# A dilated-attention and mixture-of-experts kernel: another order of the last tiles, weight sums one step earlier, last rows scaled by two engines

## The chip, the core and the metric

The kernel runs on one core of a Trainium2 chip. The core has five engines with their own instruction queues: TensorE (PE; its weight loads are shown as PEld), VectorE (DVE), ScalarE (ACT), GpSimd (POOL) and SyncE (SP). In this kernel SP issues the plain loads and stores, and POOL issues the indirect ones (gathers and scatters by a list of row numbers). The metric is the device time in microseconds of one execution.

## What is computed

Two stages follow each other. First attention over 8 batches and 8 heads, 576 positions, 64 values per head, with a plain window of 32 for half of the heads and a dilated one for the others. Its result is the input `x` of a mixture of experts: every token goes through one expert of eight, and the choice can be carried over from the token before.

```python
for b in range(B):                                   # B, S, D, E, F = 8, 576, 512, 8, 1024
    prev_e = -1
    for s in range(S):
        fresh_e = int(np.argmax(logits[b, s]))       # logits = x @ w_gate
        if s == 0 or local_gate[b, s] < 0.5:         # local_gate = sigmoid(x @ w_local)
            e = fresh_e
        else:
            e = prev_e if prev_e >= 0 else fresh_e
        prev_e = e
        p = softmax(logits[b, s])                    # in short
        h = np.maximum(x[b, s] @ w1[e], 0.0)
        out[b, s] = p[e] * (h @ w2[e])
```

All data is 32-bit floating point.

## The kernel before

**Stages.** The loop at L1155 runs the attention. Near its end the routing starts: which tokens go to which expert. When half of the batches are routed, two early units of tokens can begin; the rest of the routing runs between their matmuls. From `run_hidden(0, [])` (L1264) on, TensorE works on the experts only.

**Units.** Tokens of one expert are packed into units of fixed kinds, and only the expert numbers and token lists are data. Unit 0 is "plain" (two tiles of 128 tokens), unit 1 an early "pair". Units 2 to 17 take their kinds from `ORDER` (L85): a quad is four tiles of 128 tokens, a pair two, a full one, a half one tile of up to 64 tokens, a few one of up to 32. The n-th full in `ORDER` takes the n-th full tile in the order of the experts, and so for each kind; moving a kind within `ORDER` does not change which tokens it gets.

**One unit's work.** `features(u)` (L898) transposes the gathered tokens (TensorE L907, ScalarE copies L908). `hidden(u)` (L942) is the first layer with relu, `output(u)` (L1033) the second layer, a scaling by the gate's probability, and `send` (L1028, POOL L1029), which scatters the rows to their places in `out`. Every send writes `out`, and so waits until the send before has landed.

**Quads and pairs** use a scheme with seven block products instead of eight (Strassen's, in Winograd's form; `chain`, L916). It needs sums of blocks, made by VectorE: four of the inputs (`xc` or `xcq`, L860 to L863 by way of `sums_right`), four of the first-layer weights (`sums[0]`, L854 to L857 by way of `sums_left`), four of the second-layer weights (`sums[1]`, L860 to L863) and four of the hidden values (`hc`, L854 to L857). One operation on weights is 128x1024. The products go to three PSUM accumulators x, y, z; product 7 writes x again after x was read behind product 5 (`finish(3)`). In the first layer `finish` is VectorE L1008 and a relu (L1009, L1006), in the second VectorE L1104 or ScalarE L1101; `keep` is ScalarE L1000 or L1097.

**The order of a step.** From unit 2 on, step u issues: `hidden(u)`, `features(u+1)`, `gather(u+2)`, `output(u-1)`. So the output of a unit comes one step after its first layer. The order on every engine is the order in which the Python program issues its instructions. VectorE's sums and the routing's steps are woven between matmuls: `work_gap` is called after each group of matmuls; it runs a routing step from `waiting` if there is one, and one or two sums from the list `soon`. What is handed to `run_hidden(u, push)` or `run_output(u, push)` is put on `soon`, and what is left is issued at its end (`flush`). `both(u)` (L1241) gives the four `hc` sums of a pair or quad, woven with its four `sums[1]` unless `early_sums` (L1248) has issued those in the unit's own first layer; it does so for a quad that doesn't follow a pair.

**Weights.** There are two slots for each layer's weights, `raw1[0]`, `raw1[1]`, `raw2[0]` and `raw2[1]`, 2 MB each. Quads and the first pair use slot 0, the others slot 1. `weights(u, second)` (L803) is issued on SP's queue as soon as the slot's last user is done, and it moves nothing if the slot holds that expert already (L817).

**The first two units and the end** are written out by hand. These are the lines that the change rewrites:

```python
run_hidden(0, [])
push = features(1)
run_output(0, sums_of_weights(1, False) + push)
run_hidden(1, sums_of_weights(1, True))
```

In them the first-layer sums of unit 1 and its four `xc` sums are issued in unit 0's output, and the second-layer sums of unit 1 in its own first layer. The routing steps of that time are, in this order: `fresh` (L478 to L499), `carry` (TensorE L507, VectorE L509 and L511), `carry_over` (TensorE L517, VectorE L519 to L522), `carry_in` (TensorE L527, VectorE L528), `choose` (TensorE L533, VectorE L537 to L547), `gate` (L555 to L561), `place` (TensorE L571 and L572, VectorE L574), `lanes_of`, `matrices` (L580 to L614), `products` (TensorE L623), `count` (TensorE L640, VectorE L643 to L729), `table` (TensorE L739) and `late_tokens` (TensorE L756, VectorE L766 to L781), after which the gathers of unit 2 are issued. At the end, the last unit (17) is a quad.

Of the kernel before, what the change touches and what calls it, by code (L numbers as in the profile page):

```python
# [14 lines left out]
Act = mybir.ActivationFunctionType  # L15
Alu = mybir.AluOpType
# [8 lines left out]
D = H * DH  # L25
# [19 lines left out]
FEED = 4  # L45
# [36 lines left out]
QUADS, PAIRS, FULL, HALF, FEWS = 6, 2, 4, 1, 3  # L82
C_FULL, C_HALF, C_FEW = (2 * MOST + k * E for k in range(3))
COLS = C_FEW + E
ORDER = ("pair", "full", "quad", "few", "half", "quad", "full", "few", "quad", "full", "few", "quad", "pair", "quad",  # L85
         "full", "quad")
assert [ORDER.count(kind) for kind in ("quad", "pair", "full", "half", "few")] == [QUADS, PAIRS, FULL, HALF, FEWS]
assert 4 * QUADS + 2 * PAIRS <= C_FULL

# [133 lines left out]
def whole(ctx, tc, exact, bad, qk, v, wgl, w1, w2, con, adm, msk, qmk, out, cst, wg, ones, warm):  # L223
    nc = tc.nc
# [562 lines left out]
    else:  # L787
        kinds = list(ORDER)
    cols = dict(quad=(0, 4), pair=(0, 2) if exact else (2 * MOST - 2, -2), full=(C_FULL, 1), half=(C_HALF, 1), few=(C_FEW, 1))
# [3 lines left out]
    NU = len(units)  # L793

    def of_unit(u, what, j=0, rows=P):
        return tiles[what, units[u]["late"]][:rows, units[u]["col"] + j:units[u]["col"] + j + 1]
# [22 lines left out]
    waiting, soon = [], []  # L819
# [3 lines left out]
    def gap(add=None):  # L823
        if add is not None:
            credit[0] = min(credit[0] + add, add)
        alone = False
        while waiting and not alone and (add is None or credit[0] >= 0):
            f, cost, _ = waiting.pop(0)
            credit[0] -= cost
            if f:  # L830
                f()
            alone = add is None or not waiting or waiting[0][2]

    def work_gap(sums=True):
        before = credit[0]
        gap()
        for _ in range(len(soon) > 4 and 2 or len(soon) > 0 if sums and before - credit[0] < 1.2 else 0):
            soon.pop(0)()
# [5 lines left out]
    def flush():  # L844
        while soon:
            soon.pop(0)()

    def quarter(w, i, k, second):
        if second:
            return w[:, FK // 2 * i:FK // 2 * (i + 1), D // 2 * k:D // 2 * (k + 1)]  # L850
        return w[:, FK // 2 * i:FK // 2 * (i + 1), DK // 2 * k:DK // 2 * (k + 1)]
# [7 lines left out]
    def sums_right(to, b11, b12, b21, b22):  # L859
        return [lambda: nc.vector.tensor_tensor(to[:, 0], b12, b11, op=Alu.subtract),  # L860
                lambda: nc.vector.tensor_tensor(to[:, 1], b22, to[:, 0], op=Alu.subtract),
                lambda: nc.vector.tensor_tensor(to[:, 2], b22, b12, op=Alu.subtract),
                lambda: nc.vector.tensor_tensor(to[:, 3], b21, to[:, 1], op=Alu.subtract)]  # L863

    def sums_of_weights(u, second):

        i = units[u]["slot"]
        assert (u, second) in loads
        if second:
            return sums_right(sums[1], *(quarter(raw2[i], k, j, True) for k in range(2) for j in range(2)))  # L870
        return sums_left(sums[0], *(quarter(raw1[i], f, k, False) for f in range(2) for k in range(2)))
# [6 lines left out]
    def rows_in(u):  # L878
        return dict(half=ROW, few=FEW).get(units[u]["kind"], P)
# [153 lines left out]
    def output(u):  # L1033
        i, kind = units[u]["slot"], units[u]["kind"]
        h, w = ht.pop(u), raw2[i]
        if kind in ("half", "few"):
            rows = rows_in(u)
            parts, n = P // rows, FK * rows // P
            yp = bank([P, D // parts], "yp")
            hh = h[:, 2:2 + n // 2].rearrange("p m (c t) -> p (m c) t", t=P)  # L1040
            for m in range(FK):
                for v in range(parts):
                    nc.tensor.matmul(yp[v * rows:(v + 1) * rows],
                                     lhsT=hh[:, m % n, m // n * rows:(m // n + 1) * rows],
                                     rhs=w[:, m, v * D // parts:(v + 1) * D // parts], start=(m == 0),
                                     stop=(m == FK - 1), tile_position=(0, v * rows), skip_group_check=True)
                if m % 2:
                    yield True
            y = stage.tile([P, D], F32, name="y", bufs=3)
            nc.vector.tensor_scalar(y[:, :D // parts], yp, of_unit(u, "gate"), None, Alu.mult)  # L1050
            c = units[u]["col"] - C_HALF
            nc.gpsimd.indirect_dma_start(
                out=out.rearrange("n (v f) -> (n v) f", v=parts),
                out_offset=bass.IndirectOffsetOnAxis(ap=tiles["side"][:, c:c + 1], axis=0),
                in_=y[:, :D // parts], in_offset=None, bounds_check=parts * N - 1, oob_is_err=False)
            return
        if kind == "plain":
            for j in range(2):
                yp = bank([P, D], "yp")
                for m in range(FK):  # L1060
                    nc.tensor.matmul(yp, lhsT=h[:, m, j * P:(j + 1) * P], rhs=w[:, m], start=(m == 0), stop=(m == FK - 1))
                    if m % 2:
                        yield True
                y = stage.tile([P, D], F32, name="y", bufs=3)
                nc.scalar.activation(y, yp, Act.Copy, scale=of_unit(u, "gate", j))
                send(y, u, j)
            return
        if kind == "full":
            yp = bank([P, D], "yp")
            for m in range(FK):  # L1070
                nc.tensor.matmul(yp, lhsT=h[:, m, :P], rhs=w[:, m], start=(m == 0), stop=(m == FK - 1))
                yield True
            y = stage.tile([P, D], F32, name="y", bufs=3)
            nc.vector.tensor_scalar(y, yp, of_unit(u, "gate"), None, Alu.mult)
            send(y, u, 0)
            return
        half = D // 2
        for q in range(tiles_of(u) // 2):
            if q:
                now(sums_left(hc, *blocks(h, q)))  # L1080
            xyz = [bank([P, half], "yp") for _ in range(3)]
            ys = [stage.tile([P, D], F32, name="y", bufs=3) for _ in range(2)]

            def product(to, a, b, first):
                for m in range(FK // 2):
                    nc.tensor.matmul(to, lhsT=a[:, m], rhs=b[:, m], start=first and m == 0,  # L1086
                                     stop=(m == FK // 2 - 1), skip_group_check=True)

            def at(k):
                return ys[k // 2][:, k % 2 * half:(k % 2 + 1) * half]  # L1090

            def gate(k):
                return of_unit(u, "gate", 2 * q + k // 2)

            def keep(k, of):
                k = (0, 1, 3)[k]
                nc.scalar.activation(at(k), of, Act.Copy, scale=gate(k))  # L1097

            def finish(k, of):
                if k == 2:  # L1100
                    nc.scalar.activation(at(k), of, Act.Copy, scale=gate(k))  # L1101
                    send(ys[1], u, 2 * q + 1)
                else:
                    nc.vector.scalar_tensor_tensor(at(k), of, gate(k), at(k), Alu.mult, Alu.add)  # L1104
                    if k == 1:
                        send(ys[0], u, 2 * q)

            yield from chain((lambda j, k: blocks(h, q)[2 * j + k], lambda s: hc[:, s]),
                             (lambda k, j: quarter(w, k, j, True), lambda s: sums[1][:, s]),
                             *xyz, product, keep, finish)  # L1110
# [109 lines left out]
    def run_hidden(u, push):  # L1220
        soon.extend(push)
        for fits in hidden(u):
            work_gap(fits)
        if not units[u]["late"] and units[u]["kind"] == "pair":
            now(units[u]["sums"][:2])
        flush()
        if after[u] is not None and u >= FIRST:
            weights(after[u], False)

    def run_output(u, push):  # L1230
        soon.extend(push)
        for fits in output(u):
            work_gap(fits)
        flush()
        if after[u] is not None and u >= FIRST:
            weights(after[u], True)
# [24 lines left out]
        now(features(FIRST))  # L1261
        gather(FIRST + 1)

    run_hidden(0, [])  # L1264
    push = features(1)
    run_output(0, sums_of_weights(1, False) + push)
    run_hidden(1, sums_of_weights(1, True))
    soon.extend(units[1]["sums"][2:])
    rest = output(1)
    for k in range(FEED + 2):  # L1270
# [5 lines left out]
    for u in range(FIRST, NU):  # L1276
# [5 lines left out]
        push = sums_of_weights(u + 1, False) if is_pair(u + 1) else both(u) if u + 1 == NU else []  # L1282
# [67 lines left out]
```

## Time and profile before

| what | value |
|---|---|
| median of three runs | 658.38 us (657.23 to 659.29) |
| the profiled execution | 656.34 us, its span 654.6 us, granted clock 0.996 |
| VectorE and ScalarE busy | 323.0 us (49%), 193.7 us (30%) |
| POOL busy | 172.9 us (26%) |
| TensorE waits from 149 us to its end | four, 2.3 us together |
| DMA, mean over the span | 180 GB/s, 117.83 MB |
| weight loads issued | 36 of 2048 KB (some of them skipped), 4 of 512 KB |
| VectorE, one sum of weights (128x1024) | 1.22 us |
| VectorE, one 128x512 scaling from PSUM (L1074) | 0.75 us |
| ScalarE, one 128x256 scaling from PSUM (L1101) | 0.47 us |

The span runs from the first to the last instruction; the execution's time has 1.7 us more around it. TensorE's matmuls are pipelined and their ends are modelled, so TensorE shown busy is not TensorE at its peak. In a timeline row the first number is the start in us from the span's start, the second the length in us, and square brackets hold the idle time of that engine just before, with what ended it. In the list of waits the numbers are the total in us, how often, and the longest.

### The profile page before, as it was taken

To read this page: it belongs to the slowest core of one execution; us is meant where nothing else is said; L and a number is where in the kernel's file an instruction comes from. 1 tells how busy PE (TensorE), PEld (TensorE's weight loads), DVE (VectorE), ACT (ScalarE), POOL (GpSimd) and SP (SyncE) were. 2 spreads that over 40 slices of the span, in tenths; PEclk is the share of its full clock that TensorE was granted. 3 is DMA by queue.
4 is the path that set the end of the run, shared out by engine and by line. 5 is a ranking of instruction groups with operands and counts; after the bars stand their busy time and mean duration, and the time that the engine had idled before them with its cause. 6 is when DMAs were issued, how large, how long until landed. Compare 5 with 4: busy or idle time off the path is not lost. (4 is left out here: it accounts for less than half of the span.)

```text
span 654.6 us, 13525 instructions
## 1 busy us (share of the span) xinstructions
PE 637.7 (97%) x5602; PEld 542.1 (83%) x5602; DVE 323.0 (49%) x727; ACT 193.7 (30%) x364; POOL 172.9 (26%) x169
## 2 busy tenths in 40 slices
PE   8999999989999999999999999999999999999995
PEld 6988888878587998777889868986899888988784
DVE  3558588683696663232632363125466422742420
ACT  3555444551113322311431123212333132212210
POOL 3322213251204622051405130513531241111011
PEclk9999999999999999999999999999999999999998
DMA  8999898849101364284816170817255243404001
GB/s 314 338 298 318 296 289 309 254 123 389 55 34 49 106 253 165 93 349 153 338 60 274 49 298 10 314 45 288 81 225 212 82 159 145 161 33 157 0 31 53
DMA packets 32102, 117.83 MB, mean 180 GB/s; under 512 B 8637, under 2 KB 17053, under 8 KB 28576
## 3 DMA queue, kind: packets, MB, share of 16 engines
q1 hardware_dynamic: 25232, 97.66, 41.4%
q0 software_dynamic: 6800, 19.21, 8.6%
q8 instruction: 46, 0.75, 0.5%
q14 instruction: 24, 0.20, 0.1%
HBM read 116.86 MB, written 19.20 MB: 208 GB/s over the span
## 5 line engine op out<-in xcount | busy, mean ns | idle before, releaser
L1029 POOL DMA_INDIRECT out_dram<-y,tok x36 | 44.0, 1223 | 262.8 <-DVE y L1104 99.4
L1086 PE MATMUL yp<-sum,hc 128*128 128x256 f32 x360 | 82.7, 379 | 0.6 <-DVE hc L854 0.6
L1104 DVE SCALAR_TENSOR_TENSOR y<-yp,gate,y 128x256 f32<-128x256 f32 x45 | 21.8, 483 | 114.7 <-issue 75.7
L1086 PEld LDWEIGHTS yp<-sum,hc 128*128 128x128 f32 x360 | 68.3, 190 | 10.3 <-DVE hc L854 1.0
L995 PE MATMUL hp<-xcq,sum 128*128 128x256 f32 x288 | 64.1, 379 | 0.0
L995 PEld LDWEIGHTS hp<-xcq,sum 128*128 128x128 f32 x288 | 54.7, 190 | 7.4
L891 POOL DMA_INDIRECT xg<-xd,tok x40 | 43.5, 1089 | 62.0 <-PE tp L907 34.2
L284 POOL COPY vt<-vt 32x1040 f32<-32x1040 f32 x32 | 35.8, 1121 | 90.8 <-DMA vt<-in_v_dram 64.6
L339 PE MATMUL two<-kq 64*96 64x64 f32 x1152 | 53.5, 243 | 0.0
L339 PEld LDWEIGHTS two<-kq 64*96 64x96 f32 x1152 | 53.3, 162 | 0.1
L1008 DVE TENSOR_TENSOR hq<-hp,hq 128x512 f32<-128x512 f32 x36 | 24.8, 690 | 52.6 <-PE hp L995 52.6
L1086 PE MATMUL yp<-raw,hq 128*128 128x256 f32 x192 | 45.7, 381 | 0.0
L891 POOL DMA_INDIRECT xg<-xd,pos x40 | 40.6, 1016 | 11.8 <-issue 11.1
L995 PE MATMUL hp<-xeq,raw 128*128 128x256 f32 x192 | 43.5, 380 | 0.0
L390 PE MATMUL pv<-vt,pr 96*64 96x65 f32 x1152 | 41.2, 224 | 1.2 <-POOL vt L284 1.0
L390 PEld LDWEIGHTS pv<-vt,pr 96*64 96x64 f32 x1152 | 36.5, 137 | 5.1 <-issue 1.6
L344 DVE SCALAR_TENSOR_TENSOR pr<-two,mk 96x512 f32<-96x512 f32 x32 | 21.9, 685 | 37.8 <-ACT pr L346 26.6
L1086 PEld LDWEIGHTS yp<-raw,hq 128*128 128x128 f32 x192 | 36.1, 190 | 5.3 <-issue 0.5
L995 PEld LDWEIGHTS hp<-xeq,raw 128*128 128x128 f32 x192 | 36.2, 190 | 4.8
L1097 ACT ACTIVATE y<-yp,gate 128x256 f32<-128x256 f32 x45 | 21.3, 473 | 63.6 <-PE yp L1086 58.7
L1009 ACT ACTIVATE hq<-hq 128x512 f32<-128x512 f32 x36 | 22.7, 630 | 44.1 <-DVE hq L1008 44.1
L1101 ACT ACTIVATE y<-yp,gate 128x256 f32<-128x256 f32 x15 | 7.1, 473 | 91.2 <-PE yp L1086 91.2
(260 smaller groups left out, 1048.7 us busy)
## 6 DMA issues: line engine op xcount, KB each, us to landing
raw<-in_w_dram SPq DMA_DIRECT2D x36, 2048.0 KB
kq<-in_qk_dram SPq DMA_DIRECT2D x32, 592.0 KB
vt<-in_v_dram SPq DMA_DIRECT2D x32, 292.5 KB
xd<-x SPq DMA_DIRECT2D x16, 512.0 KB
raw<-in_w_dram SPq DMA_DIRECT2D x4, 512.0 KB
xd<-x SPq DMA_DIRECT2D x32, 32.0 KB
xg<-xd,tok POOLq DMA_INDIRECT x40, 4.0
xg<-xd,pos POOLq DMA_INDIRECT x40, 3.7
```

The lines of the kernel that those rows point to most:

```text
L284: nc.gpsimd.tensor_copy(vt[:WIN, :, 1:], vt[QB:, :, :NB - 1])
L339: nc.tensor.matmul(sc[:KW, u, k * QB:(k + 1) * QB], lhsT=kt[h, i * QB:i * QB + KW], rhs=qt[h, i * QB:(i + 1) * QB], start=bool(late), stop ...
L344: nc.vector.scalar_tensor_tensor(pr, sc[:KW, :, :w], -CEIL, mk[:, kind].unsqueeze(1).to_broadcast([KW, 2, w]), Alu.max, Alu.min)
L390: nc.tensor.matmul(to[h * QB:(h + 1) * QB], lhsT=pr[i][:, u], rhs=vt[:, u, i], start=True, stop=True, tile_position=(0, h * QB), skip_grou ...
L891: nc.gpsimd.indirect_dma_start(out=x[:rows, g], out_offset=None, in_=xd[g] if units[u]["late"] else xd[g][:EARLY * GS], in_offset=bass.Ind ...
L995: nc.tensor.matmul(to[part][:, m_], lhsT=a[:, m, kk], rhs=b[:, kk], start=first and m_ == 0 and kk == 0, stop=(kk == DK // 2 - 1), skip_gr ...
L1008: nc.vector.tensor_tensor(to, of[part], to, op=Alu.add)
L1009: nc.scalar.activation(to, to, Act.Relu)
L1029: nc.gpsimd.indirect_dma_start(out=out, out_offset=bass.IndirectOffsetOnAxis(ap=of_unit(u, "tok", j), axis=0), in_=y, in_offset=None, boun ...
L1086: nc.tensor.matmul(to, lhsT=a[:, m], rhs=b[:, m], start=first and m == 0, stop=(m == FK // 2 - 1), skip_group_check=True)
L1097: nc.scalar.activation(at(k), of, Act.Copy, scale=gate(k))
L1104: nc.vector.scalar_tensor_tensor(at(k), of, gate(k), at(k), Alu.mult, Alu.add)
```

## The change

Three things are changed. In `ORDER`, the full and few tiles from the seventh place on stand in other places: a few now comes ahead of the second full, the third few moves from the eleventh place to the fourteenth, and a full is last, after the last quad. The counts of each kind stay as they are. The four sums of unit 1's first-layer weights are put on `soon` in unit 0's first layer, behind group 4 (`FEED`), and those of its second-layer weights follow the `xc` sums in unit 0's output; nothing is handed to unit 1's first layer. Where the last unit is a full tile, VectorE scales its first 256 columns and ScalarE the other 256; other full tiles are scaled by VectorE alone, as before.

```diff
-ORDER = ("pair", "full", "quad", "few", "half", "quad", "full", "few", "quad", "full", "few", "quad", "pair", "quad",
-         "full", "quad")
+ORDER = ("pair", "full", "quad", "few", "half", "quad", "few", "full", "quad", "full", "quad", "pair", "quad", "few",
+         "quad", "full")
...
             y = stage.tile([P, D], F32, name="y", bufs=3)
-            nc.vector.tensor_scalar(y, yp, of_unit(u, "gate"), None, Alu.mult)
+            left = D // 2 if u + 1 == NU else D
+            nc.vector.tensor_scalar(y[:, :left], yp[:, :left], of_unit(u, "gate"), None, Alu.mult)
+            if left < D:
+                nc.scalar.activation(y[:, left:], yp[:, left:], Act.Copy, scale=of_unit(u, "gate"))
             send(y, u, 0)
...
-    run_hidden(0, [])
+    for k, fits in enumerate(hidden(0)):
+        if k == FEED:
+            soon.extend(sums_of_weights(1, False))
+        work_gap(fits)
+    flush()
     push = features(1)
-    run_output(0, sums_of_weights(1, False) + push)
-    run_hidden(1, sums_of_weights(1, True))
+    run_output(0, push + sums_of_weights(1, True))
+    run_hidden(1, [])
```

## The prediction

> **What bounds the kernel now.** I read the page's part 1 first, then who waited for whom with TensorE as the waiting engine, window by window, then VectorE's timeline around the waits found, and last the chain that ended last together with the timeline of the final 10 us.
>
> ```profile
> span 654.6 us, 13525 instructions
> ...
> PE 637.7 (97%) x5602; PEld 542.1 (83%) x5602; DVE 323.0 (49%) x727; ACT 193.7 (30%) x364; POOL 172.9 (26%) x169
> ```
>
> TensorE is busy 97% of the span. Its work is the same in both kernels (same matmuls, other order), so only its stalls and the two ends can give time. From 149 us to the end the waits of TensorE are these four, and from 250 to 640 us there is none:
>
> ```profile
> PE hp L995 <- DVE h L1008: 0.8, 1, 0.8
> PE yp L1086 <- DVE hc L854: 0.6, 1, 0.6
> PE ep L739 <- DVE chosen_late L729: 0.4, 1, 0.4
> PE hp L995 <- DVE sum L854: 0.4, 1, 0.4
> ```
>
> All four lie in units 1 and 2 (182 to 215 us). VectorE's timeline shows the cause of the first two (start, length, line):
>
> ```profile
> 194.82 1.22 DVE L861 TENSOR_TENSOR sum<-raw,sum 128x1024 f32<-128x1024 f32 x1
> 195.96 0.69 DVE L1008 TENSOR_TENSOR h<-hp,h 128x512 f32<-128x512 f32 x1
> 196.56 1.22 DVE L862 TENSOR_TENSOR sum<-raw 128x1024 f32<-128x1024 f32 x1
> 197.69 0.68 DVE L1008 TENSOR_TENSOR h<-hp,h 128x512 f32<-128x512 f32 x1
> ...
> 200.94 1.22 DVE L863 TENSOR_TENSOR sum<-raw,sum 128x1024 f32<-128x1024 f32 x1
> 202.08 0.69 DVE L854 TENSOR_TENSOR hc<-h 128x512 f32<-128x512 f32 x1
> ```
>
> Unit 1's second-layer weight sums (L861 to L863, 1.22 us each) stand in VectorE's queue ahead of the steps that TensorE waits for: two sums before the second L1008, one before the first hc. The tail, from the timeline of the end and the chain:
>
> ```profile
> 645.85 0.99 POOL L1029 DMA_INDIRECT out_dram<-y,tok  x1 [7.42 <-DVE y L1104]
> 646.75 0.47 ACT L1101 ACTIVATE y<-yp,gate 128x256 f32<-128x256 f32 x1 [6.43 <-PE yp L1086]
> 649.65 0.98 POOL L1029 DMA_INDIRECT out_dram<-y,tok  x1 [2.81 <-issue]
> ```
> ```profile
> 645.85 2.76 DMA out_dram<-y,tok
> ```
>
> TensorE ends at 646.71 (the last ACT starts 0.04 later). The last rows are scaled at 647.22, but their send starts only at 649.65: each send waits until the one before has landed (645.85 + 2.76 = 648.61) plus about 1 us. From the last send's start to the span's end it is 4.9 us.
>
> **Part 1, the sums one step earlier.** Nothing is added: the same eight operations of 1.22 us move. L854 to L857 go into unit 0's first layer, between the routing steps; L860 to L863 take their place in unit 0's second layer, all ahead of L710.
>
> New place of the first four: VectorE idles there, as the waits of its own rows show:
>
> ```profile
> 161.75 0.34 DVE L511 TENSOR_TENSOR_SCAN run<-row 12x96 f32<-12x96 f32 x1
> ...
> 163.32 0.16 DVE L520 COPY ends<-last 1x11 f32<-1x11 f32 x1 [1.22 <-PE last L517]
> ...
> 165.37 0.26 DVE L528 TENSOR_SCALAR run<-run,op 12x96 f32<-12x96 f32 x1 [1.69 <-PE op L527]
> 167.44 0.17 DVE L537 TENSOR_SCALAR ei<-cp 96x12 int32<-96x12 f32 x1 [1.80 <-PE cp L533]
> ```
>
> L854 starts when slot 1's first-layer weights are there. Three weight loads leave at 148.38, 149.35 and 149.97; their landing events end at 157.28, 162.21 and 167.08, one after another, and L854 needs the second. So L854 runs 162.25 to 163.47, then L519 to L522 to about 163.9, and TensorE's L527 at 165.14 doesn't wait: 1.3 us of slack. L855 ends at 165.1 (L528 needs 165.37), L856 at 166.8 (L537 needs 167.44), L857 follows L547 and ends at 169.7, L561 then at 170.9, before L571 on TensorE at 171.70. Cost: 0. If the load were late, see the third rival.
>
> Saving, followed through the queue. Before L643, VectorE now has 4 x 0.42 + 2 x 1.22 = 4.1 us of moved work instead of 4 x 1.22 + 2 x 0.42 = 5.7, so L643 starts when TensorE's count is there, about 182.7 instead of 183.23. Up to L729 the inserted work grows from 1.8 to 2.3 us (steps of 1.14, since neighbours overlap a little): L729 ends 0.06 earlier, 194.85. From there L1008, L1008, L741, L1008 follow without sums: the second L1008 ends at 196.1 instead of 198.37, and the wait of 0.85 before product 7 goes. The token steps after the third L1008 end at about 199.6 instead of 201.04; hc (L854) starts when ScalarE's last relu is done, 200.25, ends 200.94, and TensorE wants it at 201.13: the second wait goes too (0.77 between TensorE's due start 202.05 and its start at 202.82). Sum: 0.06 + 0.85 + 0.77 = 1.7 us. The gathers of unit 2 leave with the token steps, 1.4 us earlier; their second tile landed at 208.62 for transposes that begin at 209.83 and now begin at 208.1 with the landing at 207.2: covered. The wait of 0.42 on unit 2's sum moves along unchanged. Bounds: 0 and 2.1 (0.85 + 0.77 + 0.44); I take 1.7.
>
> **Part 2, the order of the tiles.** By the routing of these inputs unit 15 (few) and full 3 share an expert, and the second pair now stands between them, so slot 1's two weight arrays are loaded once more, some 4 MB. Loads cost TensorE nothing while they land before use; alone they take 8 to 9 us here (589.80 to 598.48), behind another up to 12.6 (483.17 to 495.77), and the shortest cover in the new order is unit 16's first layer: unit 13's output (12.1), few (1.9) and transposes (1.8), 15.8 us. Price 0. Few and full 2 exchange places with the same expert: no load.
>
> The new neighbourhood quad, few, quad (units 14 to 16) loads VectorE. Between unit 13's output and unit 14's it has eight sums (557.21 to 564.24 for the same eight before the old unit 16), four xcq (568.19 to 570.73) and three weight sums (570.73 to 574.33). Counted from the end of unit 13's output, T0 (558.27 there), the first two blocks end at T0 + 5.97 and + 8.5, the weight sums at + 12.1, then L1104, L857, L1104 end at + 14.3. Before, a full tile of 7.1 us gave cover; now TensorE starts output 14 at T0 + 3.6 and wants the second L1104 done at product 7, T0 + 3.6 + 10.36 = 13.96. A stall of 0.3; bounds 0 and 1.2 (one more 1.22 us sum in front). At the few-to-quad step (unit 10) the first sum is ready 6.5 us after the transposes begin, wanted at 7.1: no cost.
>
> **Part 3, the tail.** After TensorE's end the full tile has one send, and the quad's last is 7.6 us away, landed and free about 1 us before. So the wait of 649.65 - 647.22 - 0.27 goes. The scaling of 128x512 by VectorE takes 0.75 (L1074), 128x256 0.485 (L1050, the half tile), by ScalarE 0.47. In the built order of the changed kernel the ScalarE half waits for the count that the VectorE half raises, so they run one after the other: 0.04 + 0.485 + 0.04 + 0.473 = 1.04, then 0.27 to the send (645.57 to 645.85): 1.31 us after TensorE's end, where it is now 2.94. Saving 1.63. Bounds: side by side 0.8, saving 2.1; the send still behind a landing, saving 0.
>
> The Trainium skill (PSUM — Partial Sum Buffer, PSUM bank collisions raise a hardware error) says that two engines must not read one bank and quadrant at once, reads against reads included, and that the compiler therefore orders them. No run here shows a collision. By that rule the split costs more than VectorE alone (1.04 against 0.79), which speaks against it; if reads could overlap, the tail would be 0.5 us shorter.
>
> **Sum.** -1.7 + 0.3 - 1.63 = -3.0. The profiled execution took 656.34 us (span 654.6, 1.7 around it): 653.3 in its terms. The median of the runs shown, 658.38, lies 2.04 above that execution, so I forecast 655.4, own range 653.6 to 656.4.
>
> **The rivals.**
> 1. The early waits only change place, because the routing chain on VectorE (L643 to L729, nearly gapless) sets the pace anyway. For: ep waits for L729 and gains 0.06. Against: both other waits have sums directly in front. Time: 658.38 - 1.63 + 0.3 = 657.1. Chance 0.13.
> 2. The halves run side by side and the jam at unit 15 doesn't appear: 655.4 - 0.5 - 0.3 = 654.6. Against: the wait in the built order. Chance 0.10.
> 3. The slower one: the first-layer weights of slot 1 land late and L854 blocks the routing steps queued behind it (L520, L522), for which TensorE's L527 and all matmuls after it wait. It decides from a landing at 163.5 on and eats the whole gain from 163.5 + 3.0 = 166.5. With the loads interleaved, so that the second lands with the third at 167.08, TensorE loses 3.7: 659.1; 1.3 us later still it is over 0.3%. Against: the landings 5 us apart. Chance 0.07, 0.05 of it beyond 0.3%.
> 4. The reorder does not free the last send: it still waits for the quad's. Time 657.0. Against: 7.6 us between them, 3.8 us per send. Chance 0.08.
>
> **How the numbers follow.** Forecast 0.62. About 0.3% (2.0 us) is what a measurement of this kernel can tell from no change: faster means below 656.4. Faster: 0.62 + 0.10 = 0.72; within: 0.13 + 0.08 + 0.02 = 0.23; slower 0.05. The range must hold rivals 1, 2 and 4 with the spread of the runs (about 1 us either way): 652.6 to 657.8.
>
> **What would show it.** No wait of L995 on L1008 and of L1086 on hc near 198 to 203 us, L854 beginning right at 162.2, a wait of about 0.3 us in unit 14's output, the last ACT row beginning where the last DVE row ends, and 6.2 us from TensorE's end to the span's. Wrong would be: a wait of TensorE on L522 near 165 us, any wait on a weight load after 500 us, or two sends in the last 5 us.

## The result and the profile after

| what | before | after |
|---|---|---|
| median of 6 runs each, side by side | 657.87 us (657.05 to 659.66) | 654.39 us (653.10 to 656.56) |
| ratio to the kernel before, 95% interval | | 0.9945 [0.9922, 0.9967] |
| the profiled execution, its span | 656.34, 654.6 us | 656.56, 654.8 us |
| first product of unit 0's first layer (L964) | 149.49 | 153.19 |
| from there to product 2 of unit 1's output | 53.33 us | 51.69 us |
| from there to TensorE's end | 443.89 us | 443.42 us |
| TensorE's end to the last send | 2.94 us | 1.35 us |
| TensorE's end to the span's end | 7.85 us | 6.47 us |
| DMA | 117.83 MB | 122.02 MB |

The kernel became 3.5 us faster (2.2 to 5.1 by the interval). The two profiled executions do not show it at first sight: their spans are alike, because the one of after was the slowest of its six runs. The windows of the trace tell why. First the kernel before, then after; the columns are the stretch in us, its length, the busy time of PE, PEld, DVE, ACT and POOL with their counts, the granted clock, the DMA share and GB/s.

```profile
120.00:146.00 26.00, 24.32 (x473) 20.74 (x470) 19.28 (x77) 13.00 (x26) 11.18 (x15) 1.00 0.61 189
146.00:200.00 54.00, 52.52 (x334) 39.98 (x333) 35.43 (x127) 10.80 (x21) 8.05 (x6) 1.00 0.38 146
```
```profile
120.00:146.00 26.00, 23.68 (x471) 20.33 (x468) 19.36 (x77) 12.78 (x25) 9.01 (x13) 1.00 0.67 199
146.00:200.00 54.00, 53.50 (x343) 40.78 (x344) 37.89 (x130) 10.64 (x21) 8.09 (x9) 0.97 0.39 148
```

The last column but two is what to look at: in the run of after the granted clock was 0.97 between 146 and 200 us. That is the mean over one stretch of 3.41 us at half clock (147.03 to 150.44), which lies ahead of unit 0's first product and can hold TensorE up by 1.7 us; the attention stage, whose instructions the change does not touch, had run late already. Unit 0's first product came 3.7 us later. So the two kernels are compared from that product on: 505.07 us to the span's end before, 501.6 after, 3.5 us less, which agrees with the runs. The 3.5 are 1.64 in the early units, 0.47 in the long middle and 1.38 at the end.

The waits of TensorE between 150 and 250 us, in the list of after (total us, how often, longest):

```profile
PE ep L739 <- DVE chosen_late L729: 0.5, 1, 0.5
PE hp L995 <- DVE sum L854: 0.4, 1, 0.4
```

Of four rows two are left: the waits on L1008 and on `hc` are gone. From 250 us to 640 us the list is empty, as before. VectorE and TensorE at the place where the first sums went, from the timeline of after (start, length, engine, line, operation):

```profile
165.45 0.34 DVE L511 TENSOR_TENSOR_SCAN run<-row 12x96 f32<-12x96 f32 x1
165.82 1.23 DVE L854 TENSOR_TENSOR sum<-raw 128x1024 f32<-128x1024 f32 x1
...
166.82 0.17 PE L517 MATMUL last<-cst,run 12*1 12x12 f32 x1
...
167.02 0.16 DVE L520 COPY ends<-last 1x11 f32<-1x11 f32 x1
167.21 0.17 DVE L522 TENSOR_TENSOR_SCAN over<-ends 1x12 f32<-1x12 f32 x1
...
168.84 0.19 PE L527 MATMUL op<-ones,over 1*12 1x1 f32 x2
```

L854 begins as its weights are complete (the last of the load's sixteen parts landed at 165.80). L522 is done at 167.38, and L527 starts at 168.84 without a wait behind its name: the sum fitted. The tail, from the timeline of the end and then from the chain that ended last:

```profile
648.34 0.48 DVE L1075 TENSOR_SCALAR y<-yp,gate 128x256 f32<-128x256 f32 x1 [8.04 <-PE yp L1071]
648.90 0.48 ACT L1077 ACTIVATE y<-yp,gate 128x256 f32<-128x256 f32 x1 [6.96 <-DVE y L1075]
649.65 0.98 POOL L1029 DMA_INDIRECT out_dram<-y,tok  x1 [2.85 <-ACT y L1077]
```
```profile
640.57 4.20 DMA out_dram<-y,tok
...
645.81 2.73 DMA out_dram<-y,tok
...
649.65 0.98 POOL out_dram L1029
```

TensorE ends at 648.30. The ScalarE half begins 0.08 us after the VectorE half has ended (its releaser is L1075), and the last send follows the ScalarE half (releaser L1077). The chain, though, shows how little cover there was: the quad's two sends took 4.20 and 2.73 us, and the second landed only at 648.54.

### The profile page after: what moved, and what is told of

Same layout as the page of the kernel before. It is cut to its first block, busy times and chain, and to the rows that moved or that the text cites. A ratio compares the mean times of both kernels' runs of the same rounds, so it can differ in the third digit from the quotient of the medians.

```text
span 654.8 us, 13519 instructions
## 1 busy us (share of the span) xinstructions
PE 639.5 (98%) x5602; PEld 543.3 (83%) x5602; DVE 324.1 (49%) x727; ACT 194.6 (30%) x365; POOL 169.6 (26%) x169
## 2 busy tenths in 40 slices
DMA packets 32390, 122.02 MB, mean 186 GB/s; under 512 B 8669, under 2 KB 17085, under 8 KB 28608
## 5 line engine op out<-in xcount | busy, mean ns | idle before, releaser
L1029 POOL DMA_INDIRECT out_dram<-y,tok x36 | 41.0, 1140 | 244.5 <-DVE y L1107 90.5
L1107 DVE SCALAR_TENSOR_TENSOR y<-yp,gate,y 128x256 f32<-128x256 f32 x45 | 21.8, 483 | 101.2 <-issue 70.5
L1008 DVE TENSOR_TENSOR hq<-hp,hq 128x512 f32<-128x512 f32 x36 | 24.9, 691 | 42.6 <-PE hp L995 42.6
```

The source lines that it names most:

```text
L1008: nc.vector.tensor_tensor(to, of[part], to, op=Alu.add)
L1029: nc.gpsimd.indirect_dma_start(out=out, out_offset=bass.IndirectOffsetOnAxis(ap=of_unit(u, "tok", j), axis=0), in_=y, in_offset=None, boun ...
```

## The experiments

The kernel before took 658.85 us on the chip of E1 to E4, called the first here (E12 ran on it too, at 659.08), 666.41 on the second (E5 to E8) and 662.65 on the third (E9 to E11). So a kernel is compared only through its ratio to the kernel before in runs on the same chip, and, closer, by stages of its profile:

| kernel | ratio, 95% interval | unit 0's first product to unit 1's product 2 | to TensorE's end | TensorE's end to last send | to the span's end |
|---|---|---|---|---|---|
| before, after | , 0.9945 [0.9922, 0.9967] | 53.33, 51.69 | 443.89, 443.42 | 2.94, 1.35 | 7.9, 6.5 |
| E1 sums only | 0.9989 [0.9972, 1.0006] | 51.67 | 443.78 | 3.19 | 8.0 |
| E2 order and split | 0.9963 [0.9944, 0.9981] | 53.33 | 443.50 | 1.35 | 6.4 |
| E3 order only | 0.9957 [0.9932, 0.9982] | 53.32 | 443.54 | 1.08 | 6.0 |
| E4 no split | 0.9946 [0.9928, 0.9964] | 51.68 | 443.40 | 1.10 | 6.0 |
| E5 late load | 1.0006 [0.9984, 1.0029] | 52.93 | 451.19 | 1.36 | 6.2 |
| E6 two banks | 0.9932 [0.9906, 0.9958] | 51.70 | 449.55 | 0.84 | 6.1 |
| E7 sums first | 0.9934 [0.9914, 0.9954] | 51.13 | 449.30 | 1.35 | 6.5 |
| E8 two banks, sums first | 0.9929 [0.9901, 0.9958] | 51.13 | 449.58 | 0.84 | 6.2 |
| E9 after again | 0.9939 [0.9914, 0.9964] | 52.01 | 445.31 | 1.36 | 6.4 |
| E10 sums first, no split | 0.9914 [0.9880, 0.9948] | 51.12 | 447.17 | 1.07 | 6.0 |
| E11 extra sum | 0.9935 [0.9905, 0.9964] | 51.69 | 446.61 | 1.36 | 6.5 |
| E12 late load, old sums | 0.9955 [0.9937, 0.9973] | 53.33 | 443.49 | 1.36 | 6.2 |

**E1, the sums alone.** The order and the scaling of the kernel before, with only this:

```diff
-    run_hidden(0, [])
+    for k, fits in enumerate(hidden(0)):
+        if k == FEED:
+            soon.extend(sums_of_weights(1, False))
+        work_gap(fits)
+    flush()
     push = features(1)
-    run_output(0, sums_of_weights(1, False) + push)
-    run_hidden(1, sums_of_weights(1, True))
+    run_output(0, push + sums_of_weights(1, True))
+    run_hidden(1, [])
```

> The kernel before with only the sums of unit 1's weights made one step earlier; order and tail stay. My theory: the two waits of TensorE at 198 and 203 us (0.85 and 0.77) go and nothing takes their place, so the time is 1.7 us below the kernel before (ratio 0.9974), and from the first product of unit 0's first layer to product 2 of unit 1's output it is 51.7 us instead of 53.3. Tail as before: last send 2.9 us after TensorE's end. Rival (early waits only change place): the same time as before within 0.4 us (ratio 0.9994 to 1.0), with a new wait of TensorE in that stretch or after it.

The early stage took 51.67 us, 1.66 less, and the middle stayed. The ratio alone cannot tell the theory (0.9974) from the rival (0.9994 and up): both lie in its interval. The runs differ by the clock granted to them, 0.989 to 0.999, and E1's happened to have less of it (mean 0.9942, the kernel before 0.9956). A least-squares fit over the 82 runs of E1 to E4 and of the kernel before beside them, with one term for each kernel and one for (1 - clock) x 655 us, gives that last term a factor of 0.81 and puts E1 at -2.06 us (plus or minus 0.64) against the kernel before, E2 at -1.95 (0.63), E3 at -1.75 (0.66) and E4 at -3.34 (0.63). The mean clock also counts what lies behind TensorE's end, where it costs nothing: in the profile of before the only stretch at half clock begins at 649.66, and TensorE ends at 646.71. E1 and the kernel before have tails of like length, and so have E3 and E4, which differ by the same edit (1.6 us apart by the fit); these comparisons stand. E2 to E4 against the kernel before have tails 1.5 us shorter and so come out some 0.6 us too small (an estimate: 0.81 times half of 1.5). So the sums bring their 1.7, which the stage shows directly, and the first rival falls. E1 and E2 together, -4.0, make up the whole change within the intervals.

**E2, order and split without the early sums**, E1's edit undone in the changed kernel.

> The changed kernel without the early sums: new order and split last rows only. My theory: 1.4 to 2.1 us below the kernel before (ratio 0.9968 to 0.9979), all of it behind 640 us: last send 1.3 us after TensorE's end instead of 2.9; the waits of 0.85 and 0.77 near 200 us are there as before; the middle between them is within 0.5 us of the kernel before. Rival (the reorder costs a stall in units 14 to 16): a gain of only 0.3 to 1.0 us and a wait of TensorE between 550 and 600 us. Rival (the tail gains nothing, the last send still waits for the quad's): a gain of under 0.5 us.

Ratio 0.9963, 2.4 us faster. The early stage is that of before to the hundredth, and TensorE's waits from 150 to 660 us are, in E2's list:

```profile
PE hp L995 <- DVE h L1008: 0.8, 1, 0.8
PE yp L1089 <- DVE hc L854: 0.6, 1, 0.6
PE ep L739 <- DVE chosen_late L729: 0.4, 1, 0.4
PE hp L995 <- DVE sum L854: 0.4, 1, 0.4
```

The same four as before, and no fifth in units 14 to 16: the new order itself costs no stall there.

**E3, the order alone**, and **E4, the change without the split.** Both have this, E4 with the early sums, E3 without:

```diff
-            left = D // 2 if u + 1 == NU else D
-            nc.vector.tensor_scalar(y[:, :left], yp[:, :left], of_unit(u, "gate"), None, Alu.mult)
-            if left < D:
-                nc.scalar.activation(y[:, left:], yp[:, left:], Act.Copy, scale=of_unit(u, "gate"))
+            nc.vector.tensor_scalar(y, yp, of_unit(u, "gate"), None, Alu.mult)
```

> The kernel before with only the new order: VectorE alone scales the last rows (128x512). My theory: the order carries the whole tail gain and the split costs 0.25: the last send starts 1.06 us after TensorE's end (0.04 + 0.75 + 0.27) instead of 1.3 with the split, unless the quad's landing is what releases it; time 1.6 to 2.3 us below the kernel before, and the same or 0.25 below the run with the split. Rival (the split carries a part of the gain): 0.2 us or more slower than the run with order and split.

> The changed kernel with the last rows scaled by VectorE alone. My theory: the ScalarE half starts only when the VectorE half has ended, so leaving the split out brings the last send from 1.35 to about 1.06 us after TensorE's end; time 0.25 us below the changed kernel, or the same where the quad's last landing releases the send. Rival (the halves overlap in effect and the split pays): 0.3 us or more slower than the changed kernel.

E4's tail, from its timeline, with TensorE's end at 645.90:

```profile
643.48 0.99 POOL L1029 DMA_INDIRECT out_dram<-y,tok  x1 [4.32 <-issue]
...
645.93 0.75 DVE L1074 TENSOR_SCALAR y<-yp,gate 128x512 f32<-128x512 f32 x1 [8.04 <-PE yp L1071]
647.00 0.98 POOL L1029 DMA_INDIRECT out_dram<-y,tok  x1 [2.53 <-DVE y L1074]
```

One operation of 0.75 us in place of 0.48 + 0.08 + 0.48: the last send comes 1.10 us after TensorE's end, 0.25 earlier than with the split; in E3 1.08. To the span's end it is 6.0 us in both against 6.4 and 6.5. The order has all of the tail's gain, and the split takes 0.25 of it back at the last send. Whether it also costs the other 0.2 is not shown: from the last send to the span's end the runs with this split take 4.87 to 5.15 us, those with VectorE alone 4.90 to 4.96. The times can't show so little: E4's ratio is that of the changed kernel.

**E5, a late load**, for the third rival: what happens when the sum's weights come late.

```diff
         if n == NPB + 1:
             weights(0, True)
-            weights(1, False)
...
     weights(1, True)
+    weights(1, False)
```

> The changed kernel with the first-layer weights of slot 1 asked for behind its second-layer weights, so that they land some 5 us later (about 14 to 17 us after TensorE begins unit 0's first layer, instead of 12.6). Third rival of the prediction as a theory: the first sum then stands in VectorE's queue waiting for the landing and blocks the routing steps queued behind it (L520, L522), for which TensorE's L527 and all matmuls after it wait; TensorE loses 3 to 4.5 us there and the time is 3 to 4.5 us above the changed kernel. Rival (the scheduled place has slack enough, or the sums don't block): the same time as the changed kernel within 0.5 us, no wait of TensorE at L527.

The gain is gone: ratio 1.0006. The timeline of E5, at the same place as that of after above (unit 0's first product at 154.36):

```profile
169.61 1.23 DVE L854 TENSOR_TENSOR sum<-raw 128x1024 f32<-128x1024 f32 x1 [2.65 <-DMA raw<-in_w_dram]
...
170.76 0.15 DVE L520 COPY ends<-last 1x11 f32<-1x11 f32 x1
...
170.94 0.17 DVE L522 TENSOR_TENSOR_SCAN over<-ends 1x12 f32<-1x12 f32 x1
...
171.26 0.18 PE L527 MATMUL op<-ones,over 1*12 1x1 f32 x2 [1.19 <-DVE over L522]
```

VectorE stands 2.65 us before the sum, waiting for the weights; L520, whose input had come from TensorE at 168.15, is queued behind; and TensorE waits 1.19 us for L522. The early stage is 1.24 us longer than in the changed kernel. The mechanism is the rival's. The size in this profile is smaller than expected: the load landed 4.9 us behind the one before it (164.70 and 169.59), as expected, but only 15.2 us after unit 0's first product, 2.6 later than in after (12.6).

The runs lost more than that 1.24. The fit used for E1, over the 63 runs of this chip (factor 0.82), puts E5 at -0.42 us (0.80) against the kernel before and E6 to E8 at -3.90 to -4.09. The profile has two stretches at half clock; these rows of its windows lie inside them (columns as above):

```profile
150.70:154.00 3.30, 3.30 (x32) 1.34 (x31) 1.66 (x3) 0.52 (x2) 1.45 (x2) 0.50 0.99 266
300.90:304.20 3.30, 3.30 (x10) 2.59 (x9) 1.60 (x3) 0.47 (x1) 0.75 (x2) 0.50 0.21 79
```

The second, 300.86 to 304.28, is why the middle is 1.6 us longer than in E6, whose waits of TensorE there are the same. The first, 150.68 to 154.09, seems to hide a part of the loss: the first of the three loads left at 151.01, unit 0's first product came 3.35 us behind it, and in the eight profiles without a stretch at half clock near that place it is 1.1 to 1.7. With these the sum would have begun 16.9 to 17.5 us after the first product, and TensorE would have waited 2.9 to 3.4 us (an estimate, by the threshold of 14.06 worked out below). That is about what the runs lost, since by stages E6 to E8 are 0.4 to 0.9 us better than the changed kernel; no profile shows it.

**E12, the late load with the sums in their old places**, to see whether the transfers' order costs something by itself.

> The load of slot 1's first-layer weights asked for late, as in the run with the late load, but the sums of unit 1's weights left in their old places; new order and split tail stay. The run with the late load gave up about 4 us against the changed kernel, of which its profile shows 1.24 at L527. My theory (only the blocked routing steps cost): no wait at L527, the late load by itself is free, and the time is that of the run with order and split without the early sums, ratio to the kernel before 0.9963 (0.9944 to 0.9981). Rival (the late load itself costs, by the order of the transfers and not by what stands behind the sum): ratio 0.998 to 1.001, with a longer stage before unit 0's first product or a new wait of TensorE behind it.

Ratio 0.9955, early stage 53.33, no wait at L527: the late load is free where no sum stands in front of the routing. It was another chip than E5's.

**E6, two banks for the last output**: two products of 256 columns each, VectorE scales the first while TensorE makes the second, ScalarE scales that.

```diff
+            if u + 1 == NU:
+                for c in range(2):
+                    cols = slice(c * D // 2, (c + 1) * D // 2)
+                    yp = bank([P, D // 2], "yp")
+                    for m in range(FK):
+                        nc.tensor.matmul(yp, lhsT=h[:, m, :P], rhs=w[:, m, cols], start=(m == 0), stop=(m == FK - 1))
+                        yield True
...
```

> The changed kernel with the last full tile's output as two products of 256 columns in two PSUM banks: VectorE scales the first half while TensorE computes the second, ScalarE scales the second. My theory: one bank shared by the two engines is what made the halves run one after the other; with two banks 0.04 + 0.47 + 0.27, so the last send starts about 0.8 us after TensorE's end instead of 1.35, and the time falls by up to 0.5 us. TensorE's own time is the same or up to 0.3 longer (16 matmuls of 256 columns instead of 8 of 512). Rival (the quad's last landing releases the send, not the rows): ScalarE ends 0.5 us earlier, the send starts at the same distance from the quad's landing, gain under 0.2 us.

```profile
647.87 0.99 POOL L1029 DMA_INDIRECT out_dram<-y,tok  x1 [2.78 <-issue]
648.46 0.48 DVE L1080 TENSOR_SCALAR y<-yp,gate 128x256 f32<-128x256 f32 x1 [4.63 <-PE yp L1075]
651.96 0.47 ACT L1078 ACTIVATE y<-yp,gate 128x256 f32<-128x256 f32 x1 [6.48 <-PEq L218]
652.71 0.98 POOL L1029 DMA_INDIRECT out_dram<-y,tok  x1 [3.84 <-ACT y L1078]
```

In E6's timeline the VectorE half (L1080) is done three microseconds before the ScalarE half begins, 0.09 after TensorE's end at 651.87. The last send is 0.84 us after TensorE's end, as expected, and TensorE's output takes 7.07 us against 7.03. But the end of the span is 6.1 us after TensorE's end, 0.4 less than in after and no better than without the split (E3 and E4): in this profile what is won at the send is given back in its landing. Nor could the send have gone much sooner: the quad's second send had landed only at 651.68, and where the rows are long ready a send starts 1.04 us after the landing before it (before: 648.61 and 649.65).

**E7, the second-layer sums ahead of the token sums**, and **E8**, E6 and E7 together.

```diff
-    run_output(0, push + sums_of_weights(1, True))
+    run_output(0, sums_of_weights(1, True) + push)
```

> The changed kernel with unit 1's four second-layer weight sums put ahead of the token sums of unit 1 in unit 0's output. My theory: the last wait of TensorE in that stretch (0.5 us on L729, which ends late because two weight sums of 1.22 us stand among the routing steps from L643 to L729) becomes shorter or goes, since only two steps of 0.42 us then stand there: 0.3 to 0.5 us below the changed kernel. Rival (the chain from L643 to L729 is bound by TensorE and its round trips, not by the sums): the wait of 0.5 stays, same time within 0.2 us. A third outcome: the token sums come late for unit 1's first products, with a new wait of TensorE there, and the time is 0.3 us or more above.

> The changed kernel with both further edits, last output in two PSUM banks and the weight sums ahead of the token sums. My theory: the two gains lie in different stretches and add, 0.5 to 1.0 us below the changed kernel. Rival (neither end is what binds): within 0.3 us of the changed kernel.

In E7's list of waits from 150 to 250 us one row is left:

```profile
PE hp L995 <- DVE sum L854: 0.4, 1, 0.4
```

The wait on L729 is gone, and the early stage is 0.56 us shorter (51.13 against 51.69). By stages E7 is 0.5 us better than the changed kernel; by ratios (0.9934, E8 0.9929, the changed kernel 0.9945 and 0.9939 on other chips) this is not resolved.

**E9 to E11, side by side on a third chip**: the changed kernel again (E9), E7's edit without the split (E10), and the changed kernel with one of unit 16's sums made twice (E11):

```diff
         push = sums_of_weights(u + 1, False) if is_pair(u + 1) else both(u) if u + 1 == NU else []
+        if u + 3 == NU:
+            push = push[:1] + push
```

> The changed kernel itself once more, as the measure for the runs beside it on the same chip. My theory: ratio to the kernel before 0.9945 as measured at first (0.9922 to 0.9967), tail from TensorE's end to the end of the span 6.4 to 6.5 us, no TensorE wait in units 14 to 16. Rival: what the first profile showed was luck, and a wait of some 0.3 us in unit 14's output comes and goes.

E9 repeats the gain (0.9939), and it shows something that the first profile did not. From its timeline, with unit 0's first product at 150.76:

```profile
165.08 1.23 DVE L854 TENSOR_TENSOR sum<-raw 128x1024 f32<-128x1024 f32 x1 [1.73 <-DMA raw<-in_w_dram]
...
166.42 0.17 DVE L522 TENSOR_TENSOR_SCAN over<-ends 1x12 f32<-1x12 f32 x1
...
166.74 0.18 PE L527 MATMUL op<-ones,over 1*12 1x1 f32 x2 [0.26 <-DVE over L522]
```

The third rival's wait is here in the changed kernel itself, 0.26 us long. Fifteen of the load's sixteen parts had landed by 162.48, the last at 165.06. The loads before and behind it have a last part as late (2.4 and 2.6 us).

> The changed kernel with unit 1's second-layer weight sums ahead of the token sums in unit 0's output, and the last rows scaled by VectorE alone. My theory: 0.55 us saved before 202 us (the wait on L729 goes) and 0.25 at the last send: 0.5 to 1.0 us below the changed kernel (ratio to it about 0.9988), and the best of all versions run. Rival (the end of the span hangs on landings, not on the send): only 0.3 to 0.6 below.

E10 has the lowest ratio of all, 0.9914, its median 0.9 us below E9's; the intervals overlap. By stages it gains 0.89 in the early units (0.32 of that is the wait above and its neighbours, which E9 had on this chip) and 0.4 at the end, and in its profile waits of 1.5 and 0.3 us in middle quads take that back. So by its interval it beats the kernel before; that it beats the changed kernel is likely and not shown.

> The changed kernel with one more VectorE sum (128x1024, 1.22 us, the first of unit 16's first-layer sums made twice; the result is the same) ahead of the others in unit 14's output. In the changed kernel's trace the second L1107 of that output ended at 569.06 and TensorE's product behind it started at 569.20, so the jam on VectorE missed TensorE by 0.14 us. My theory (the jam is real and nearly decides): TensorE waits 1.0 to 1.1 us on L1107 there, and the time is 0.7 to 1.2 us above the changed kernel. Rival (TensorE has more room there, since products go on in other banks): no wait over 0.2 us, same time.

Unit 14's output on VectorE and TensorE, from the timelines of after and then of E11:

```profile
567.46 1.21 DVE L857 TENSOR_TENSOR sum<-raw,sum 128x1024 f32<-128x1024 f32 x1
568.59 0.47 DVE L1107 SCALAR_TENSOR_TENSOR y<-yp,gate,y 128x256 f32<-128x256 f32 x1
...
569.20 1.91 PE L1089 MATMUL yp<-sum,hq 128*128 128x256 f32 x8
```
```profile
568.71 1.21 DVE L857 TENSOR_TENSOR sum<-raw,sum 128x1024 f32<-128x1024 f32 x1
569.84 0.87 DVE L1107 SCALAR_TENSOR_TENSOR y<-yp,gate,y 128x256 f32<-128x256 f32 x2
...
570.37 1.99 PE L1089 MATMUL yp<-sum,hq 128*128 128x256 f32 x8 [1.03 <-DVE y L1107]
```

The second L1107 starts 1.25 us later, and TensorE waits 1.03 us for it. So the jam is real, and the changed kernel misses it by little more than a tenth of a microsecond. In the times the difference (0.9935 against 0.9939) is not resolved.

## Why the prediction came out right, point by point

**What bounds the kernel.** TensorE, and its stalls in units 1 and 2 and the tail: yes. All of the gain that could be placed lies there.

**Part 1, forecast 1.7, measured 1.64 (E1: 1.66).** The waits of 0.85 and 0.77 went and none came in their place. Only the 0.06 at L739 did not come: it starts 45.31 us after unit 0's first product, before 45.26. With two weight sums among the routing steps up to L729 that wait stayed; E7, where two shorter token sums stand there, removes it.

**The slack of the first sum, and the third rival.** The prediction let the rival decide from a landing at 163.5, 14.0 us after unit 0's first product. E9 lost 0.26 with the sum beginning at 14.32 and E5 1.19 at 15.25: both put the threshold at 14.06. The working was right, and the chance of 0.07 was not idle: in E9 a late part of the load was enough to cross it, at a price of 0.26 us. The landings 5 us apart were right too (E5: 4.9). What the prediction took as fixed is how far unit 0's first product lies behind the issue of the loads: 1.1 us in before, 2.1 in after and 3.35 in E5, and each us of that is slack for the sum.

**Part 2, forecast a stall of 0.3, measured none.** This is the step that failed, by its size; the mechanism, the jam on VectorE, is there. The prediction had the second L1107 done 14.3 us after the end of unit 13's output and wanted at 13.96. In after that end is at 555.08 (0.22 after its last matmul starts, as in the prediction), the operation is done at 569.06 (13.98) and TensorE comes to it at 569.20 (14.12): 0.32 earlier and 0.16 later, so the stall missed by 0.14. No profile of the new order has a TensorE wait in unit 14's output but E11's, whose 1.03 is the margin of 0.14 taken from one more sum. The extra reload cost nothing, as forecast: 4.19 MB more, and no wait on a weight load after 500 us. The middle was even 0.2 to 0.5 us shorter in the four profiles of the new order from the first chip and in after (443.40 to 443.54, against 443.89 and 443.78 in the old order). Where these tenths come from in 440 us was not found out.

**Part 3, forecast 1.63, measured 1.59 to the last send and 1.38 to the end.** The halves ran one after the other with the lengths of the forecast (1.35 us against 1.31), and undoing the split gave back the 0.25 that the prediction charged for it. The Trainium skill (PSUM — Partial Sum Buffer, PSUM bank collisions raise a hardware error) says that two engines must not read one bank and quadrant at once; the ScalarE row beginning 0.08 us after the VectorE row's end agrees, and no run here tried the two reads at once. The cover was misjudged: the quad's last send was to be landed and free a microsecond before, at 3.8 us per send. The quad's first send took 4.20 us instead of 2.73 and the next started 1.04 after it, so the last landed at 648.54. The step from a landing to the next send has been as short as 0.77 us (before: 636.68 to 637.45) and is 1.04 where the rows were long ready, so that landing would have let the last send go at 649.31 to 649.58; it went at 649.65. The fourth rival, that the send still waits for the quad's, fell by 0.1 to 0.3 us and not by one.

**The sum.** Forecast -3.0, measured -3.5. The terms differ by +0.06 (part 1), -0.77 (the stall that did not come, and the shorter middle) and +0.25 (the tail). Of the 1.0 us between the forecast of 655.4 and 654.39, 0.5 is that the kernel before took 657.87 in these runs and not 658.38. The second rival's forecast, 654.6, is nearer to the median of 654.39 than the likeliest one's 655.4, but by luck: only its second half (no stall from the jam) is right, and its first (side by side) is wrong.

## What to carry to other kernels

A sum or copy that is put early into an in-order queue is free only while its input lands before the steps queued behind it are due: work out that moment, and leave room for one late part of a transfer. At the end of a kernel look at what the last transfer must follow, and give the last piece one send with work ahead of it that covers the landing of the send before. Splitting one small operation over two engines did not pay here, where the two took turns: one operation of 0.75 us beat two of 0.48.

## What the runs showed of the hardware

One of the sixteen parts of a transfer can come much later than the rest, and everything waits for it. In E9 it is 2.6 us for a weight load (162.48 and 165.06); the cause was not found. In after it is 1.5 us for the quad's first send (643.30 and 644.77), which made a send of 2.7 us one of 4.2. There the trace has a candidate: a packet of 16 KB on the queue that the page calls "instruction" took one of the sixteen DMA engines from 641.87 to 643.32. In all twelve profiles of the new order such a packet begins 1.0 to 2.0 us after one of the quad's two sends, and that send takes 3.7 to 4.4 us. In the two of the old order (before and E1) none begins in the first 2.4 us of the last two sends, and they take 2.7 to 3.0. No run moved the packet, so that it is the cause is not shown.

Three chips ran the same kernel in 658.85, 662.65 and 666.41 us. On the second chip all four profiles, and on the third that of E10, show TensorE waits in the outputs of the quads between 285 and 370 us, 2.1 us at one place in E6 and 1.5 in E10, which are in no profile from the first chip; their cause is open.

The granted clock, between 0.985 and 0.999 over a span, goes with differences between single runs of one kernel that are larger than the whole change (E8: 659.25 us at 0.997, 667.15 at 0.985). In the profiles it is either full or half, and the stretches at half clock are 3.41 us long or two or three times that. Ahead of TensorE's end they lie in the attention or just ahead of unit 0's first product (after, E1, E2, E5, E8 and E12) and once in the middle (E5); the stage from unit 0's first product to unit 1's product 2 has none in any profile.
